# The last 16 rows of four late stores, sent apart from the other 112, in an attention backward kernel

## The chip, the core and the metric

The kernel runs on one core of one Trainium2 chip. The metric is device time in microseconds (us) for one execution, and the median of several runs counts. A core has five engines that run instructions (TensorE = PE, VectorE = DVE, ScalarE = ACT, GpSimd = POOL, SyncE = SP), and 16 DMA engines that move data between the chip's HBM and its on-chip memory SBUF, which has 128 rows (partitions). This document calls one DMA engine a **lane**.

## What is computed

Attention for one query per head, forward and backward, with 2 x 32 = 64 heads, 8,192 keys of 128 elements each, all bf16. The forward pass is

```
scores = jnp.einsum("bhqd,bhkd->bhqk", q, k) * scale
p = _softmax(scores, axis=-1)
return jnp.einsum("bhqk,bhkd->bhqd", p, v)
```

and the reference returns its output and the gradients for q, k and v from `jax.vjp`, given `grad_out`. With one query per head the gradients of K and V are outer products, as large as K and V themselves: for each head 2 MB of K and 2 MB of V are read, and 2 MB of dK and 2 MB of dV are written. In all, 268 MB are read and 268 MB are written.

## The kernel before

**Tiles.** One tensor of one head (8,192 x 128 bf16, 2,048 KB) lies in SBUF as 128 rows of 16 KB each, and in HBM it is seen in the same way (`k_v`, `dk_v` and so on, L81 to L84). Ten such places form a ring (L108). A load fills a place with K or V (L121, issued by SP). Later VectorE writes the gradient over the loaded data (`outer`, L317: four pieces for each place), and a store sends the place to HBM; then the next load can use it.

**Order.** The loop runs over heads h and, within one head, over eight steps j. While TensorE transposes K and V of head h (L144), ScalarE copies the transposed pieces out of PSUM (L151) and TensorE forms the scores (L160). In the same steps the outer products of the head before, p = h - 1, are made and stored: dV of p (w = 0) is stored in step j = 3 and dK of p (w = 1) in step j = 7, by L448. The order of each engine's instructions is that of the program text (`tc.manual_schedule`).

**Which queue stores.** As long as loads remain to be issued (`todo`) or p is under LAST = 60, ACT issues the store. From head 60 on, SP does:

```
store(p, j // 7, by=nc.scalar if todo or p < LAST else nc.sync)
```

So (60, 0), (60, 1), (61, 0), (61, 1) and (62, 0) go from SP as whole stores of 128 rows (L361). dK of head 62 and both gradients of head 63 go in halves by `store_half` (L365), each 128 rows of 8 KB. The last outputs, `out_0` and dq, are two small stores by ACT (L498).

**Six other stores** (`is_rare`, L134: every tenth store of a head, up to head 55) are cut into small transfers that POOL issues (`store_by_fifteen`, L335). A transfer of 44 rows (rows 52 to 95) comes first; then, four times, come 3 rows (L348, from rows 20 to 31), 4 rows (L349, from rows 0 to 15), 8 rows (L350, from rows 96 to 127), 4 rows (L351, from rows 32 to 47) and 2 rows (L354, from rows 16 to 19 and 48 to 51). Transfers of a few bytes (`turn`, L326) lie between them. Beside each of five of these stores, SP issues one transfer of a single row of 32 bytes (`between`, L114).

**Semaphores.** Each DMA issued by SP or ACT signals its end on one of eight semaphores, which the framework gives out in turn. The trace shows their numbers: 100, 102, 103, 104, 115, 116, 117, 118. The framework puts a wait ahead of an issue whose semaphore may still belong to an earlier DMA in flight.

Of the kernel before, what the change touches and what calls it, by code (L numbers as in the profile page):

```python
# [23 lines left out]
RING = 10  # L24
AWAY = 10
LAST = 60


@with_exitstack
def kernel(  # L30
# [11 lines left out]
    nc = tc.nc  # L42
    B, H, Sq, D = q.shape
    Sk = k.shape[2]
    P = nc.NUM_PARTITIONS
# [37 lines left out]
    dk_v = out_2.rearrange("b h (p n) d -> (b h) p n d", n=NT)  # L83
    dv_v = out_3.rearrange("b h (p n) d -> (b h) p n d", n=NT)  # L84
# [17 lines left out]
    heads = [Head() for _ in range(BH)]  # L102
# [9 lines left out]

    def between(out):
        nc.sync.dma_start(out=out, in_=q_rows[0:1, 0:16])  # L114

    todo = [(h, w) for h in range(BH) for w in range(2)]

# [5 lines left out]
    def cleared(h, w):  # L123
        for a in away:
            a[0] -= 1
        if is_rare(h, w):
            away.append([AWAY, heads[h].kv[1 - w]])
        elif todo:
            load(heads[h].kv[1 - w])
        if todo and away and away[0][0] == 0:  # L130
            between(spare[0:1, 480:496])
            load(away.pop(0)[1])

    def is_rare(h, w):  # L134
        return (2 * h + w) in range(RARE // 2, RARE * len(EXTRA), RARE)
# [199 lines left out]
    def store_by_fifteen(h, w):  # L335

        dst, src = (dv_v, dk_v)[w][h], heads[h].kv[1 - w]

        def rows(lo, n, step=4, size=8192):
            own = slice(lo, lo + step * (n - 1) + 1, step)  # L340
            nc.gpsimd.dma_start(out=dst[own], in_=src[own], max_dma_last_dim=size)  # L341

        rows(52, 44, 1)
        turn(5)
        for r, e in enumerate(EXTRA[(2 * h + w) // RARE]):
            rows(20 + r, 3)  # L348
            rows(r, 4, size=16384)  # L349
            rows(96 + r, 8)  # L350
            rows(32 + r, 4, size=16384)  # L351
            if e:
                turn(e)
            rows(16 + r, 2, step=32)  # L354
            for n in (9, 8) if e == 2 else ((3 - e) % 16,):
                turn(n)

    def store(h, w, a=0, b=NT, by=None):
        if is_rare(h, w):
            return store_by_fifteen(h, w)  # L360
        (by or nc.scalar).dma_start(  # L361
            out=(dv_v, dk_v)[w][h][:, a:b, :], in_=heads[h].kv[1 - w][:, a:b, :]
        )

    def store_half(h, w, i):  # L365
        store(h, w, 2 * i * CH, 2 * (i + 1) * CH, nc.sync)
# [22 lines left out]
    for i in range(2):  # L389
# [3 lines left out]
            out=qz[i][:, 0 : 4 * BH].rearrange("p (h z) -> p h z", z=4)[:, :, 3], in_=tps[:]  # L393
# [7 lines left out]
    with tc.manual_schedule():  # L401
        for place in ring:
            load(place)
        for h in range(BH):
# [5 lines left out]
            for j in range(NS):  # L410
# [35 lines left out]
                if x and j in (3, 7) and not (last and j == 7):  # L446

                    store(p, j // 7, by=nc.scalar if todo or p < LAST else nc.sync)  # L448
                    cleared(p, j // 7)
# [15 lines left out]
        h, x = BH - 1, heads[BH - 1]  # L465
# [64 lines left out]
```

## Time and profile before

| what | value |
|---|---|
| three runs | 1280.69, 1276.09, 1275.3 us; median 1276.09 us |
| the profiled execution | 1275.3 us, of which the span of its instructions is 1273.5 us |
| busy share of the span | PE 85%, PE weight loads 57%, DVE 70%, ACT 76%, POOL 8% |
| DMA | 44,552 packets, 539.01 MB, mean 423 GB/s |
| packets on SP's queue (q1), ACT's (q10), POOL's (q0) | 20,026, 16,736, 7,648 |
| loads, median from issue to landing | 38.8 us (K), 38.6 us (V) |
| whole stores by SP (5), from issue to landing | 20.3 us |
| half stores by SP (6), from issue to landing | 10.7 us |

The span runs from the first instruction to the last. "Landing" is the moment when a DMA's semaphore is complete. The trace has sixteen landing marks for each such DMA, one for each lane, so that it can be seen how far the lanes are apart. It also has a record of each packet (start, duration, size, queue), without the number of the lane. In a busy lane the next packet starts 3 or 4 ns before the recorded end of the one before, and with this the packets can be linked into sixteen chains.

### The profile page before, as it was taken

To read this page: it belongs to the slowest core of one execution; us is meant where nothing else is said; L and a number is where in the kernel's file an instruction comes from. 1 tells how busy PE (TensorE), PEld (TensorE's weight loads), DVE (VectorE), ACT (ScalarE), POOL (GpSimd) and SP (SyncE) were. 2 spreads that over 40 slices of the span, in tenths; PEclk is the share of its full clock that TensorE was granted. 3 is DMA by queue.
4 is the path that set the end of the run, shared out by engine and by line. 5 is a ranking of instruction groups with operands and counts; after the bars stand their busy time and mean duration, and the time that the engine had idled before them with its cause. 6 is when DMAs were issued, how large, how long until landed. Compare 5 with 4: busy or idle time off the path is not lost.

```text
span 1273.5 us, 31594 instructions
## 1 busy us (share of the span) xinstructions
PE 1083.4 (85%) x13444; PEld 721.0 (57%) x13444; DVE 891.6 (70%) x1574; ACT 971.1 (76%) x1134; POOL 106.9 (8%) x194
## 2 busy tenths in 40 slices
PE   5999998769988869888888888888888888898895
PEld 4666665546655546555565555555555555565563
DVE  1888886658766658776667677677676776776685
ACT  5898886758877759777778777777786777787785
POOL 1001110001110000211000121000111000022000
PEclk9999998889998989899889998999898999898997
DMA  9999999999999999999999999999999999999997
GB/s 393 419 428 429 425 427 427 428 430 428 426 426 426 430 429 427 427 427 426 430 429 427 430 426 426 428 429 428 426 424 426 426 428 429 425 414 426 428 415 333
DMA packets 44552, 539.01 MB, mean 423 GB/s; under 512 B 10682, under 2 KB 10682, under 8 KB 10682
## 3 DMA queue, kind: packets, MB, share of 16 engines
q1 hardware_dynamic: 20026, 285.22, 52.7%
q10 hardware_dynamic: 16736, 239.15, 44.2%
q0 software_dynamic: 7648, 12.61, 2.6%
q8 instruction: 105, 1.72, 0.5%
q14 instruction: 37, 0.30, 0.1%
HBM read 268.47 MB, written 268.47 MB: 422 GB/s over the span
## 4 chain that ended last, share of the span: by engine, by line
DMA 75%; PE 16%; ACT 4%; DVE 3%; issue 1%; ACTq 0%; SPq 0%; DVEq 0%
DMA ring<-in_k_dram 51%; DMA ring<-in_v_dram 15%; PE tp L144 9%; DMA out_dram<-ring 7%; ACT ev L151 4%; PE raw L160 2%; PE acc L285 2%; DVE ring L317 2%; PE turned L177 2%; DMA spare<-in_q_dram 1%; DMA nat<-in_grad_out_dram 1%; DVE rawsb L171 1%; DVE ev L149 0%; PE misc L229 0%; ACT E_f L218 0%
## 5 line engine op out<-in xcount | busy, mean ns | idle before, releaser
L151 ACT CAST ev<-tp 128x1024 bf16<-128x1024 f32 x960 | 936.3, 1017 | 288.4 <-PE tp L144 237.8
L144 PE MATMUL tp<-ident_bf,ring 128*128 128x128 bf16 x8192 | 661.0, 226 | 151.0 <-DMA ring<-in_k_dram 67.4
L144 PEld LDWEIGHTS <-ring 128*128 128x128 bf16 x8192 | 516.2, 101 | 370.1 <-issue 239.8
L317 DVE TENSOR_TENSOR ring<-qd,dS 128x2048 bf16<-128x2048 bf16 (+1 forms) x256 | 305.4, 1214 | 0.3 <-PE acc L285 0.3
L317 DVE TENSOR_TENSOR ring<-qd,P 128x2048 bf16<-128x2048 bf16 x255 | 305.3, 1218 | 0.1
L171 DVE COPY rawsb<-raw 128x512 f32<-128x512 f32 x127 | 87.8, 692 | 236.2 <-PE raw L160 235.0
L285 PE MATMUL acc<-ring,wz 128*32 128x512 bf16 x2048 | 211.2, 404 | 1.4 <-DVE wz L232 1.4
L160 PE MATMUL raw<-ev,qz 128*4 128x512 bf16 x2048 | 205.1, 390 | 0.1
L341 POOL DMA_DIRECT2D out_dram<-ring x126 | 70.7, 562 | 959.8 <-DVE ring L317 610.8
L177 PE MATMUL turned<-ident_f,rawsb 128*128 128x128 f32 x512 | 90.7, 305 | 11.6 <-DVE rawsb L171 10.2
L149 DVE CAST ev<-tp 128x1024 bf16<-128x1024 f32 x64 | 78.4, 1225 | 16.3 <-PE tp L144 15.7
L160 PEld LDWEIGHTS <-qz 128*4 128x4 bf16 x2048 | 46.6, 81 | 56.4 <-issue 6.2
L177 PEld LDWEIGHTS turned<-ident_f,rawsb 128*128 128x128 f32 x512 | 60.6, 154 | 26.7 <-DVE rawsb L171 25.3
L285 PEld LDWEIGHTS <-wz 128*32 128x32 bf16 x2048 | 52.7, 93 | 30.6 <-issue 3.0
L229 PEld LDWEIGHTS misc<-ld,ones_f 128*128 128x128 f32 x256 | 38.6, 190 | 15.2 <-DVE ld L256 10.9
L229 PE MATMUL misc<-ld,ones_f 128*128 128x1 f32 x256 | 46.1, 249 | 0.4 <-DVE ld L256 0.4
L209 DVE TENSOR_REDUCE gm<-misc 1x1 f32<-1x128 f32 x64 | 17.8, 279 | 38.5 <-PE misc L207 38.5
L331 POOL DMA_DIRECT2D spare<-in_q_dram x56 | 33.0, 588 | 120.3 <-DMA out_dram<-ring 102.3
L203 DVE TENSOR_REDUCE mp<-turned 128x1 f32<-128x64 f32 x64 | 14.1, 220 | 25.1 <-PE turned L177 23.9
L215 DVE TENSOR_SCALAR negm<-misc 128x1 f32<-128x1 f32 x64 | 9.8, 153 | 24.1 <-PE misc L213 24.1
L213 PE MATMUL misc<-gm,ones_f 1*128 1x1 f32 x128 | 24.2, 256 | 0.0
L213 PEld LDWEIGHTS misc<-gm,ones_f 1*128 1x128 f32 x128 | 18.7, 183 | 6.8 <-issue 0.4
(46 smaller groups left out, 283.1 us busy)
## 6 DMA issues: line engine op xcount, KB each, us to landing
out_dram<-ring ACTq DMA_DIRECT2D x114, 2048.0 KB, 19.3
ring<-in_k_dram SPq DMA_DIRECT2D x64, 2048.0 KB, 38.8
ring<-in_v_dram SPq DMA_DIRECT2D x64, 2048.0 KB, 38.6
out_dram<-ring SPq DMA_DIRECT2D x5, 2048.0 KB, 20.3
out_dram<-ring SPq DMA_DIRECT2D x6, 1024.0 KB, 10.7
out_dram<-ring POOLq DMA_DIRECT2D x6, 704.0 KB, 15.2
out_dram<-ring POOLq DMA_DIRECT2D x48, 64.0 KB, 21.1
out_dram<-ring POOLq DMA_DIRECT2D x24, 128.0 KB, 22.3
```

The lines of the kernel that those rows point to most:

```text
L144: nc.tensor.matmul(tp[:, i, :], lhsT=x.kv[w][:, n, :], rhs=ident_bf[:], start=True, stop=True)
L149: nc.vector.tensor_copy(out=ev[:], in_=tp[:])
L151: nc.scalar.copy(out=ev[:], in_=tp[:])
L160: nc.tensor.matmul(raw[32 * k : 32 * k + 4, :], lhsT=qz[w][:, at : at + 4], rhs=evs[k // 2][:, 4 * (k % 2) : 4 * (k % 2) + 4, :].rearrange ...
L171: copy(out=x.raw[:], in_=raw[:])
L177: nc.tensor.transpose(out[:, i], x.raw[:, i * P : (i + 1) * P], ident_f[:])
L213: nc.tensor.matmul(mb, lhsT=ones_f[0:1, :], rhs=x.gm[:], start=True, stop=True)
L229: nc.tensor.matmul(x.lsum, lhsT=ones_f[:], rhs=x.ld[:, w : w + 1], start=True, stop=True)
L285: nc.tensor.matmul(acc[32 * g : 32 * g + 32, :], lhsT=wz[w][:, n // 4, at : at + 32], rhs=rows[:, n : n + 4, :].rearrange("p n d -> p (n d)"),
L317: nc.vector.tensor_tensor(out=x.kv[1 - w][:, n : n + size, :].rearrange("p n (d t) -> p n d t", t=2), in0=row.unsqueeze(1).to_broadcast([P ...
L331: nc.gpsimd.dma_start(out=two(spare[0:n, :])[:, :, i : i + 2], in_=two(q_rows[0:n, :])[:, :, 0:2])
L341: nc.gpsimd.dma_start(out=dst[own], in_=src[own], max_dma_last_dim=size)
```

## The change

The stores of heads 60 and 61 by SP (four in all) no longer go as one transfer of 128 rows. Rows 0 to 111 go as one transfer, and rows 112 to 127 follow in small ones: dV (w = 0) in four transfers of four rows each, dK (w = 1) in two transfers of eight rows each. The rows of one small transfer lie 4 or 2 rows apart (112, 116, 120, 124 for the first of dV). All are issued by SP, directly behind one another. The bytes and everything else stay as they are.

```diff
+UNEVEN = {(60, 0): 4, (60, 1): 8, (61, 0): 4, (61, 1): 8}
...
+    def in_parts(engine, out, in_, n):
+        engine.dma_start(out=out[: P - 16], in_=in_[: P - 16])
+        step = 16 // n
+        for i in range(step):
+            own = slice(P - 16 + i, P, step)
+            engine.dma_start(out=out[own], in_=in_[own])
...
     def store(h, w, a=0, b=NT, by=None):
         if is_rare(h, w):
             return store_by_fifteen(h, w)
-        (by or nc.scalar).dma_start(
-            out=(dv_v, dk_v)[w][h][:, a:b, :], in_=heads[h].kv[1 - w][:, a:b, :]
-        )
+        dst, src = (dv_v, dk_v)[w][h], heads[h].kv[1 - w]
+        if (h, w) in UNEVEN:
+            in_parts(by, dst, src, UNEVEN[h, w])
+        else:
+            (by or nc.scalar).dma_start(out=dst[:, a:b, :], in_=src[:, a:b, :])
```

## Prediction

> **What bounds the kernel.** I read the page first. The DMA row is full in nearly every slice:
>
> ```profile
> DMA  9999999999999999999999999999999999999997
> GB/s 393 419 428 429 425 427 427 428 430 428 426 426 426 430 429 427 427 427 426 430 429 427 430 426 426 428 429 428 426 424 426 426 428 429 425 414 426 428 415 333
> DMA packets 44552, 539.01 MB, mean 423 GB/s; under 512 B 10682, under 2 KB 10682, under 8 KB 10682
> ```
>
> The bytes bound the span, and the change moves as many. It touches only what SP issues from 1218.8 us on, when all loads are issued (the last at 1211.0). Nothing waits for those stores but the end of the program, so the question is when the last lane is done. The stretches of the tail (columns: stretch, length, busy us of PE, PEld, DVE, ACT, POOL, clock, DMA share, GB/s):
>
> ```profile
> 1230.00:1240.00 10.00, 9.39 (x119) 6.64 (x119) 7.36 (x16) 8.92 (x12) 0.00 (x0) 1.00 0.99 419
> 1240.00:1245.00 5.00, 5.00 (x74) 2.91 (x71) 4.93 (x9) 4.36 (x6) 0.00 (x0) 1.00 0.71 301
> 1245.00:1255.00 10.00, 8.62 (x106) 5.43 (x104) 8.71 (x17) 8.48 (x15) 0.00 (x0) 1.00 0.98 412
> 1255.00:1260.00 5.00, 2.03 (x18) 0.67 (x18) 4.61 (x8) 4.97 (x19) 0.00 (x0) 0.70 0.77 321
> 1260.00:1267.00 7.00, 2.29 (x10) 1.96 (x10) 2.08 (x4) 2.02 (x8) 0.00 (x0) 0.50 1.02 426
> 1267.00:1274.00 7.00, 0.00 (x0) 0.00 (x0) 0.00 (x0) 0.00 (x0) 0.00 (x0) 0.50 0.31 124
> ```
>
> At 1240 to 1245, 1255 to 1260 and after 1267 the share falls: some lanes are out of work while others are behind. The sixteen landing marks tell which. The last load (issued 1211.0) lands in five lanes at 1218.64 to 1221.64, in three at 1223.17 to 1226.05, and in eight at 1230.45 to 1233.43. The last half store (issued 1261.53) lands in eight lanes at 1267.56 to 1267.79 and in the eight others at 1270.55 to 1272.50. That last mark ends the span 1.0 us later, at 1273.5. The eight late lanes never pause after 1218: the slowest goes from 1233.43 in steps of 4.8 to 4.9 us per whole store and 2.4 to 2.5 per half. The eight early ones do: the half store issued at 1258.87 lands there 3.7 us later, so they stood idle. A row of 16 KB takes 611 ns in a lane (median of 17,024 packets on q1).
>
> **What a late lane gains.** A whole store gives each lane 8 rows, one of 112 rows gives 7 (112 = 16 x 7). Over four stores a lane without extras saves 4 x 0.611 = 2.44 us: the slowest would land at 1270.06. The 64 rows set free go to the lanes that carry the small transfers.
>
> **Which lanes carry them** is the main choice, since no 4- or 8-row transfer from SP stands in this trace. The nearest rows are POOL's. I linked the packets of the last rare store into chains. Each transfer of n rows ran in n lanes, one row in each, and always in the same lanes: 4 rows (L349, L351) in a set F, 3 rows (L348) in a set T, 8 rows (L350) in a set E, all disjoint. One lane N got none. Of the five most early lanes 2 are of F, 1 of T and 2 of E; the next three are the other 2 of F and N; the eight late ones are 2 of T and 6 of E. SP's own one-row transfer (L114) ran all five times, the last at 1046.2 us, in one of the most early lanes. I take it as the first lane, and the order of the lanes as that of the rows: F (rows 0 to 15), N, T (20 to 31), E (96 to 127). Then a 4-row transfer fills F, and an 8-row one fills F, N and T. In rows over four stores, F gets 28 + 4 + 2 + 4 + 2 = 40, N and T get 28 + 2 + 2 = 32 as before, E gets 28.
>
> [...]
>
> So the six late lanes of E gain 2.44 us, but **the two late lanes of T gain nothing**. In the marks of the last half store these two stand at 1271.87 and 1270.55. That leaves 1272.50 - 1271.87 = 0.63 us of gain.
>
> **What the extra issues cost SP.** Four issues become 16. Two issues in a row are 0.40 us apart (1218.84 and 1219.24), so 12 x 0.40 = 4.8 us, hidden under SP's waits for VectorE: only stores stand behind them, and the window from 1205 shows
>
> ```profile
> SPq L361 <- DVE ring L317: 27.8, 8, 9.3
> ...
> SPq L361 <- DMA ring<-in_k_dram: 7.4, 1, 7.4
> ...
> SPq L361 <- DMA ring<-in_v_dram: 4.0, 1, 4.0
> ```
>
> The lower two lines matter more. A store has no use for a load of another head: (60, 0) waits for the load issued at 1179.24, because both use semaphore 102. The eight semaphores go round in order, so 16 issues take two rounds, and the new ones meet loads in flight. I follow them. (60, 0): main part 1218.84 [102], parts at 1219.2 [103], 1223.7 [104, held by the load that lands at 1223.65], 1224.1 [115], 1228.6 [116, load landing 1228.54]. (60, 1): main part 1229.0 [117] in place of 1219.24, parts 1233.5 [118, load landing 1233.43] and 1233.9 [100]. (61, 0) needs 102 again, thus the landing of the first main part in the slowest lane, 1233.43 + 7 x 0.611 = 1237.71: issued 1237.8 in place of 1227.02, its parts to 1239.4. (61, 1): 1242.1 in place of 1233.87 (one more main part, 4.28 us later). (62, 0) waits for (61, 0), last in the slower T lane with its 7 + 9 + 7 rows: about 1246.9 in place of 1243.58. From the half store at 1250.35 on, data are late again and all is as before.
>
> Does this starve a lane? An idle lane's first packet comes 0.83 us after the issue (1243.58 to 1244.41), and the mark 0.35 us after the last packet. The late lanes: the first of them ends its (60, 1) rows at 1230.1 + 14 x 0.611 = 1238.65, and the next main part is there at 1237.8 + 0.83 = 1238.63; so none pauses. The F lanes do wait, until 1238.6. From there they have 7 + 4 + 7 + 2 = 20 rows (12.2 us), the 8 of (62, 0) (4.9 us) and six halves (2.47 us each, 14.8 us) without a pause: 1238.6 + 31.9 + 0.35 = 1270.9 instead of 1267.6. They use up their slack, and stay 1.0 us below the T lane.
>
> **Sum.** Last marks: E 1270.06, F 1270.9, T 1271.87. The end moves by -0.63 us: span 1272.9, and the profiled execution's 1275.3 becomes 1274.7. The median of the runs shown is 0.8 us above that execution, so I predict 1276.09 - 0.6 = 1275.5 us. About 0.5% (6.4 us) is what a measurement of this kernel can tell from no change, so this is within it.
>
> [...]
>
> **Rivals.**
> (a) The 8-row transfers fall on the eight early lanes alone, or the T lanes are not as late as I read them. Then all late lanes gain 2.44 us and the end is F's 1270.9: -1.6 us, 1274.5. If moreover the semaphores hold nothing up, F ends at about 1270.2 at most: -2.3, 1273.8. For it: the marks split eight to eight. Against it: the chains.
> (b) Nothing moves: the small transfers are spread over all 16 lanes, 32 rows' worth in each as before. 1276.1. For it: no SP transfer of 4 rows has been seen; against it: POOL's.
> (c) **Slower: the rows cost more.** With 7 rows in each lane a lane no longer reads the same SBUF rows as in a whole store, and two lanes may meet in one group of rows. Price per row from the nearest packets: 0 from POOL's 2-row transfers, which ran in foreign lanes (of all 1,152 packets of 8 KB on q0, 7 took over 330 ns against 309); 19 ns from lane N, the slowest, whose mean is 630 ns; 407 ns if each were like the longest one at 1245 to 1260 (1,018 ns). Times 28 rows (32 in T): 0, +0.6 and up to +13 us. It decides from 0.63/32 = 20 ns per row on. I take 0, the packets that did just this; as a case of its own, 100 ns, +3 us net, 1279. [...]
> (d) Slower too: the extra rows fall on a late lane, 40 rows in place of 32, +4.9 us at its end, 1281. Against it: L114's lane was early five times.
>
> **Chances.** Forecast 0.52, (a) 0.17, (b) 0.08, (c) 0.13, (d) 0.07, other 0.03. The three runs spread over 5.4 us, so a median may lie 2 us off. The range 1272.8 to 1280.2 holds forecast, (a), (b) and most of (c). Faster by over 0.5% (below 1269.7) 0.02; slower by over 0.5% (above 1282.5), from the far ends of (c) and (d), 0.06; within 0.92.
>
> **What would show it.** q1 grows by 64 packets to 20,090 (each small transfer adds a 4-byte packet per lane it uses) at equal MB. SP's issue times are those listed; (61, 0) near 1237.8 confirms the semaphores. Four-row transfers have landing marks of four early lanes. The last half store's latest mark is near 1271.9, two lanes unmoved and six 2.4 us earlier. The row packets stay at 611 ns. I am wrong if the latest mark is below 1271 (a), at 1272.5 (b), or if the median packet of the main parts is above 630 ns (c).

## The result, and the profile after

The changed kernel takes **1292.49 us** (median of 6 runs, 1292.01 to 1293.06) against 1275.28 us before (6 runs, 1275.07 to 1280.69): a ratio of 1.0127, 95% interval 1.0111 to 1.0143, or 17.2 us slower. The forecast was 1275.5 us, the range ended at 1280.2. The profiled execution has a span of 1290.6 us.

The page of the changed kernel, the rows that answer to the first ones shown of before:

```profile
DMA  9999999999999999999999999999999999999976
GB/s 395 421 428 427 427 425 427 428 432 425 427 428 427 428 429 428 428 426 426 429 429 428 428 426 427 429 428 428 422 425 428 427 428 429 416 426 424 417 264 267
DMA packets 44616, 539.01 MB, mean 418 GB/s; under 512 B 10746, under 2 KB 10746, under 8 KB 10746
...
q1 hardware_dynamic: 20090, 285.22, 52.5%
```

The bytes are the same and q1 has the 64 packets more that were forecast. The loss is all in the last two slices, at 264 and 267 GB/s. The stretches of the tail in the changed kernel (columns as in the prediction):

```profile
1230.00:1240.00 10.00, 9.54 (x123) 6.72 (x124) 7.36 (x15) 8.85 (x11) 0.00 (x0) 1.00 0.88 304
1240.00:1245.00 5.00, 5.00 (x75) 2.96 (x73) 4.93 (x9) 4.42 (x5) 0.00 (x0) 1.00 0.96 324
1245.00:1255.00 10.00, 8.62 (x103) 5.40 (x100) 8.71 (x17) 8.48 (x16) 0.00 (x0) 1.00 0.75 242
1255.00:1260.00 5.00, 1.10 (x17) 0.34 (x16) 4.61 (x8) 4.97 (x19) 0.00 (x0) 0.80 0.24 56
1260.00:1267.00 7.00, 2.30 (x10) 1.96 (x10) 1.80 (x4) 1.75 (x7) 0.00 (x0) 0.50 0.03 7
1267.00:1274.00 7.00, 0.00 (x0) 0.00 (x0) 0.00 (x0) 0.00 (x0) 0.00 (x0) 0.50 0.90 337
1274.00:1280.00 6.00, 0.00 (x0) 0.00 (x0) 0.00 (x0) 0.00 (x0) 0.00 (x0) 0.50 1.00 421
```

Read the last two columns against each other. Two things are wrong here, and they look different. From 1230 to 1245 the lanes are busy (0.88 and 0.96) but move little for it (304 and 324 GB/s; before, 419 at a share of 0.99 and 301 at 0.71): **busy and slow**. From 1255 to 1267 they are **idle** (0.24, then 0.03), while before they were at 0.77 and 1.02; the compute engines finish as they did before. The stores that should fill this stretch come after 1267, when nothing else is left to do.

Why they come late is in the waits of SP's queue in the changed kernel, from 1205 us on (columns: waiting line, what it waited for: us in all, times, longest):

```profile
SPq L125 <- DMA out_dram<-ring: 10.8, 2, 7.1
SPq L125 <- DMA out_dram<-rows: 10.5, 1, 10.5
...
SPq L376 <- DMA out_dram<-rows: 0.2, 1, 0.2
```

L125 is a small part of a store, and it waits 10.5 us for a store of `rows`: one of the two last small stores (`out_0` and dq) that ACT issues. The trace gives the numbers. ACT's two stores, issued at 1264.46 and 1265.32, carry semaphores 103 and 104. SP's last small part of (61, 1) also needs 103: it is issued at 1266.24, behind the landing of ACT's store at 1266.23. (62, 0) needs 104 and goes at 1267.14 (before: 1243.58), and the six half stores stand behind it in SP's queue, issued from 1267.59 to 1273.50 instead of 1245.85 to 1261.53. The last lands at 1289.36.

The framework had given ACT's two stores their numbers amid SP's: SP's issues at 1238.93 and 1239.32 carry 102 and 115, and 103 and 104, which lie between, went to ACT. Before, the same could be seen: SP's stores at 1258.87, 1259.61 and 1261.53 have 102, 104 and 116, and ACT's two have the missing 103 and 115. But only two SP issues stood behind the first of them there, and the turn of eight did not come round. In the changed kernel fourteen do. ACT's stores take two of the eight numbers, so six SP issues go by before the turn comes back to ACT's two, and the other eight are held behind them: one small part, (62, 0) and six halves. The twelve added issues do not do this by their count, since all of them stand ahead of the half stores, among which ACT's numbers fell before: **the place of ACT's two numbers in the turn has moved forward.**

The "busy and slow" part is in the packets: a row of 16 KB on q1 takes a mean of 738 ns from 1218 to 1262 us (the longest 2,688) against 616 before (the longest 1,102).

So there are two theories beside the forecast. **W**, the hold: stores wait in SP's queue for ACT's last two. **R**, the rows: a transfer of 112 rows makes rows dear (G and S below are forms of it, N its rival). A third suspect, the twelve extra issues themselves, is tested too (theory I in the expectations).

### The profile page after: what moved, and what is told of

Its sections match the earlier page's. It is cut to its first block, busy times and chain, and to the rows that moved or that the text cites. A ratio compares the mean times of both kernels' runs of the same rounds, so it can differ in the third digit from the quotient of the medians.

```text
span 1290.6 us, 31608 instructions
## 1 busy us (share of the span) xinstructions
PE 1089.5 (84%) x13444; PEld 722.3 (56%) x13444; DVE 891.1 (69%) x1574; ACT 971.9 (75%) x1134; POOL 106.9 (8%) x194
## 3 DMA queue, kind: packets, MB, share of 16 engines
q1 hardware_dynamic: 20090, 285.22, 52.5%
## 4 chain that ended last, share of the span: by engine, by line
DMA 72%; PE 17%; ACT 4%; DVE 3%; issue 1%; ACTq 0%; SPq 0%; DVEq 0%
DMA ring<-in_k_dram 54%; DMA ring<-in_v_dram 11%; PE tp L155 9%; DMA out_dram<-ring 7%; ACT ev L162 4%; PE acc L296 3%; PE raw L171 3%; DVE ring L328 2%; PE turned L188 2%; DMA nat<-in_grad_out_dram 1%; DVE rawsb L182 1%; PE misc L240 0%; DVE ev L160 0%; ACT E_f L229 0%; PE misc L314 0%
## 5 line engine op out<-in xcount | busy, mean ns | idle before, releaser
L328 DVE TENSOR_TENSOR ring<-qd,P 128x2048 bf16<-128x2048 bf16 x255 | 305.3, 1218 | 0.1
L188 PE MATMUL turned<-ident_f,rawsb 128*128 128x128 f32 x512 | 88.5, 299 | 11.5 <-DVE rawsb L182 10.1
L240 PEld LDWEIGHTS misc<-ld,ones_f 128*128 128x128 f32 x256 | 38.6, 190 | 15.3 <-DVE ld L267 11.6
```

The source lines that it names most:

```text
L188: nc.tensor.transpose(out[:, i], x.raw[:, i * P : (i + 1) * P], ident_f[:])
L240: nc.tensor.matmul(x.lsum, lhsT=ones_f[:], rhs=x.ld[:, w : w + 1], start=True, stop=True)
L328: nc.vector.tensor_tensor(out=x.kv[1 - w][:, n : n + size, :].rearrange("p n (d t) -> p n d t", t=2), in0=row.unsqueeze(1).to_broadcast([P ...
```

## The experiments

Medians are compared with runs of the kernel before that were made with them on the same chip (median 1275.36 to 1275.59). Only the edits are shown; those marked "from the change" start from the changed kernel, the others from the kernel before.

### The hold: rows_by_sp, before_rows_by_sp, head60_only, fours_only

**rows_by_sp**, from the change, lets SP issue the last two small stores itself, behind all others; **before_rows_by_sp** does so in the kernel before.

```diff
-            nc.scalar.dma_start(out=dst, in_=rows[:])
+            nc.sync.dma_start(out=dst, in_=rows[:])
```

> The changed kernel, with the two last small stores (out_0 and dq) issued by SP behind its half stores instead of by ACT. Theory W (SP's store waits for ACT's two small stores because they were given the semaphore numbers 103 and 104 before SP's later stores came to them): no store of SP has to wait for them now, the half stores are issued when their data are ready (1250 to 1261.5), and the 10.5 us wait is gone; with rows of 611 ns the time is 1274.7 us. Theory R (the rows of a 112-row transfer cost more: packets of 16 KB took 707 ns on average from 1218 to 1245 in the changed kernel, 616 in the one before) acting beside W: up to 28 rows times 0.17 us, 1280. R alone, or theory I (twelve more issues on SP hold the queue by themselves): the time stays at 1288 or more, and the gap in the DMA share from 1255 to 1267 stays.

> The kernel before with the same move of the two small stores to SP: the control for the run with the changed kernel. All theories: within 1.5 us of the kernel before (1275.3), a little slower, since the two small stores now stand behind the last half store in SP's queue.

Measured: rows_by_sp 1282.37 us, ratio 1.0052 [1.0035, 1.0068]; before_rows_by_sp 1275.4 us, 0.9996 [0.9986, 1.0005]. The edit by itself does nothing, and takes 10.1 us off the changed kernel (1292.49 to 1282.37). The same stretches in rows_by_sp:

```profile
1230.00:1240.00 10.00, 9.54 (x127) 6.62 (x125) 7.33 (x17) 8.52 (x11) 0.00 (x0) 1.00 0.98 333
...
1255.00:1260.00 5.00, 1.38 (x16) 0.34 (x16) 4.62 (x8) 4.97 (x19) 0.00 (x0) 0.67 0.89 285
1260.00:1267.00 7.00, 2.30 (x10) 1.96 (x10) 1.46 (x4) 1.32 (x6) 0.00 (x0) 0.50 1.00 420
```

The empty stretch from 1255 to 1267 is gone: W is right. The slow one is still there, 333 GB/s at a share of 0.98, and 6.8 us remain (1282.37 - 1275.59); R had allowed for less, up to 1280 us.

The 10.1 and the 6.8 us are not the prices of two separate costs. With the hold, the lanes had run dry before 1267 (a share of 0.03), so nearly all that slow rows had cost by then was hidden under it. An estimate for the hold alone, with the prediction's own terms: (62, 0) is issued at 1267.14, when ACT's store allows it, and 1267.14 + 0.83 + 4.9 + 14.8 + 0.35 = 1288.0 for the last landing, against 1289.36 measured. The hold alone would thus make about 16 of the 17.2 us; take it away, and 6.8 us of slow rows come into view. No run has the hold without the 112-row transfers.

**head60_only** and **fours_only**, from the change, cut only two of the four stores, so that fewer issues stand behind ACT's numbers.

```diff
-UNEVEN = {(60, 0): 4, (60, 1): 8, (61, 0): 4, (61, 1): 8}
+UNEVEN = {(60, 0): 4, (60, 1): 8}     # head60_only
+UNEVEN = {(60, 0): 4, (61, 0): 4}     # fours_only
```

> The change for head 60 alone: six more issues in place of twelve. In the program the semaphores of ACT's two small stores come round again at the last two half stores of SP. Theory W: these two are issued only when ACT's small stores have landed, about 1266.2 and 1267.1 in place of 1259.6 and 1261.5; the lanes are empty by then, 0.83 + 2 x 2.47 + 0.35 us later the end is near 1272.6, so the time is 1274 to 1277 though the wait is there. Theory I: half of the loss, 1284. Theory R: half of the row price, at most 1278, and no store is held up.

> The change for the two dV stores alone (8 more issues, all of four rows). The semaphores of ACT's small stores come round at the first half store of head 63, so the last four half stores of SP are held. Theory W: they are issued from 1266.2 on, and four half stores of 2.47 us end at 1266.2 + 0.83 + 9.9 + 0.35 = 1277.3, 4.8 us later than before: 1280. Theory I: two thirds of the loss, 1287. Theory R: half the row price, 1276 to 1279, with no store held.

Measured: 1278.8 us (1.0027 [1.0017, 1.0037]) and 1283.59 us (1.0047 [1.0019, 1.0075]). The hold shrinks with the number of issues, but it is still there: two half stores are held in head60_only, issued at 1270.29 and 1270.77, four in fours_only, issued from 1266.28 to 1268.88. That fits the count: eight and ten SP issues stand behind ACT's numbers there, and six go by in each. Both times are above what W alone had forecast (at most 1277, and 1280), so here too something else costs. From head60_only's waits of SP's queue:

```profile
SPq L376 <- DMA out_dram<-rows: 11.7, 1, 11.7
```

Here ACT's store was issued at 1264.03 and had landed in fifteen lanes by 1267.52, but in the sixteenth at 1270.22; SP went on at 1270.29. That one lane, 2.7 us behind the other fifteen, held both half stores.

### The issues: tiny_twelve

The kernel before with whole stores, and twelve transfers of 32 bytes by SP at the places of the small parts.

```diff
+        for i in range({(60, 0): 4, (60, 1): 2, (61, 0): 4, (61, 1): 2}.get((h, w), 0)):
+            at = 16 * len(tiny)
+            tiny.append(at)
+            nc.sync.dma_start(out=small[0:1, at : at + 16], in_=q_rows[0:1, 0:16])
```

> The kernel before, with whole stores, and twelve transfers of 32 bytes more on SP at the places of the changed kernel's small transfers (4, 2, 4 and 2 behind the stores of heads 60 and 61). In this program the numbers of ACT's two small stores fall late, and none of SP's stores comes back to them. Theory W and theory R: no hold and no slow row; SP issues its stores later by the turn of the semaphores alone, within 1.5 us of the kernel before. Theory I (the number of issues): the 7 us that remained with the small stores on SP, or more, so 1282 or later.

Measured: 1276.29 us, ratio 1.0007 [0.9998, 1.0016]. Twelve issues and their turn of semaphores cost 0.9 us, no more than the measurement can tell from nothing. ACT's stores have the numbers 117 and 100 here, and two SP issues stand behind the first of them, as before. So the count of issues does not move ACT's place. It stays at two in main_only, seven_eighths, col_halves and by_columns below as well; it moves in every kernel that adds row transfers of 16 KB a row and leaves ACT's stores to ACT. There six SP issues stand behind it in row_halves, even_odd, the two crossed kernels and sixteens (so none is held by ACT's stores), and eight, ten and fourteen in head60_only, fours_only and the change. How the framework chooses the place is not shown. The whole stores went out at 1229.26, 1239.17, 1243.69 and 1248.54; the prediction had 1229.0, 1237.8, 1242.1 and 1246.9 by following the semaphores.

### The rows: main_only, seven_eighths, sixteens

**main_only** issues the 112-row transfers alone. **seven_eighths** leaves out as many bytes the other way: all 128 rows, 56 of 64 columns. **sixteens** sends the 16 rows as one transfer, by count one row for each lane. All are from the change.

```diff
         engine.dma_start(out=out[: P - 16], in_=in_[: P - 16])
-        step = 16 // n
-        for i in range(step):
-            own = slice(P - 16 + i, P, step)
-            engine.dma_start(out=out[own], in_=in_[own])      # main_only: no more than the line above
-        engine.dma_start(out=out[: P - 16], in_=in_[: P - 16])
+        engine.dma_start(out=out[:, :56, :], in_=in_[:, :56, :])     # seven_eighths: this alone
-UNEVEN = {(60, 0): 4, (60, 1): 8, (61, 0): 4, (61, 1): 8}
+UNEVEN = {(60, 0): 16, (60, 1): 16, (61, 0): 16, (61, 1): 16}     # sixteens
```

> Only the 112-row transfers: rows 112 to 127 of the four stores are left out (64 rows of 16 KB are not written), so there is no extra issue and no wait for ACT's small stores. If a row of a 112-row transfer costs no more than one of a whole store, each lane does 4 rows less, 2.44 us, and the time is 1272.9. Theory R (0.17 us more per row, from the packet durations of the changed kernel): 28 x 0.17 = 4.8 us more than that, 1277 to 1278, and from 1224 to 1245 the DMA share stays near 1 while the rate falls from 419 to about 330 GB/s.

> The control for the run with 112 rows alone: the same four stores move the same number of bytes, but as 128 rows of which each leaves out its last eighth (14 KB of 16 KB; what is left out is not written). No theory gives it a row price: 1272.9, packets of 14 KB in about 0.54 us, and a rate above 410 GB/s up to 1240. Theory R is that the difference between the two runs is the price of 112 rows; without R they are equal.

> The same split, but the last 16 rows go as one transfer in all 16 lanes, so each lane keeps its 8 rows; 4 more issues, and no store comes back to the semaphores of ACT's small stores. Without a row price: 1275.3, as before. Theory R: 28 rows of the main parts at 0.17 us more, +4.8, and the 16-row transfers more per row than that, since all of their rows lie close together in SBUF: 1280 to 1288. Theory W alone: 1275.3.

Measured: main_only 1285.21 us (1.0074 [1.0059, 1.0089]), seven_eighths 1273.61 us (0.9987 [0.9977, 0.9996]), sixteens 1287.27 us (1.0081 [1.0063, 1.0099]). With the same bytes and the same four issues, **the shape of 112 rows costs 1285.21 - 1273.61 = 11.6 us**. R's forecast for main_only, 1277 to 1278 us, was some 7 us short: it had spread the price evenly over the lanes. The stretches of main_only, then those of seven_eighths:

```profile
1230.00:1240.00 10.00, 9.54 (x128) 6.57 (x125) 7.33 (x17) 8.37 (x11) 0.00 (x0) 1.00 0.97 331
...
1245.00:1255.00 10.00, 8.18 (x99) 5.24 (x95) 8.72 (x17) 8.49 (x16) 0.00 (x0) 1.00 0.97 292
```

```profile
1230.00:1240.00 10.00, 9.30 (x122) 6.59 (x119) 7.36 (x16) 8.92 (x12) 0.00 (x0) 1.00 0.90 377
...
1245.00:1255.00 10.00, 8.78 (x109) 5.50 (x105) 8.72 (x15) 8.49 (x14) 0.00 (x0) 1.00 0.97 406
```

At a share of 0.97 in both, one moves 292 GB/s and the other 406. In main_only the loss falls on two lanes: the last half store lands in fourteen lanes from 1271.5 to 1273.9, in the two others at 1278.54 and 1282.55. It was also held up itself: SP waited 7.0 us for its semaphore, until the slowest lane of (62, 0) had landed, at 1267.73 (before: 1257.70).

### Which rows: row_halves, even_odd, col_halves, by_columns

Theory G says that lanes slow each other when, in a transfer of another shape than a whole store's, they read SBUF rows that lie together; which rows lie together was my supposition, shown by no run. The test cuts each of the four stores in two, by rows, by every second row, and by columns; by_columns makes the change's twelve small transfers out of columns.

```diff
+        for own in (slice(0, 64), slice(64, 128)):                    # row_halves
+        for own in (slice(0, 128, 2), slice(1, 128, 2)):              # even_odd
+            engine.dma_start(out=out[own], in_=in_[own])
+        for own in (slice(0, 32), slice(32, 64)):                     # col_halves
+            engine.dma_start(out=out[:, own, :], in_=in_[:, own, :])
+        engine.dma_start(out=out[:, :48, :], in_=in_[:, :48, :])      # by_columns
+        step = 16 // n
+        for i in range(step):
+            own = slice(48 + i * n, 48 + (i + 1) * n)
+            engine.dma_start(out=out[:, own, :], in_=in_[:, own, :])
```

> Each of the four stores goes as two transfers of 64 rows, rows 0 to 63 and then rows 64 to 127: 4 issues more than before, every row stored, rows of 16 KB as in a whole store, and in each transfer 4 rows for each of 16 lanes. No store meets a number that one of ACT's last small stores holds. [...] Theory N (only a row number that is no power of two, 7 for each lane, is dear, or only the small transfers): 1275.5 us.

> As with the two row halves, but the two transfers of a store hold its even and its odd rows. [...] A weaker form of G, in which it only matters that a transfer as a whole spreads over all rows: about as before, below 1279 us. Theory N: 1275.5 us.

> The control to the two row halves: each of the four stores goes as two transfers of all 128 rows, columns 0 to 31 and 32 to 63, packets of 8 KB; 4 issues more than before, all bytes stored. Each lane keeps its 8 rows. Theory G and theory N: 1275.5 us, 8 KB packets near 309 ns. If it is only the number of larger transfers that costs, it is as slow as the row halves.

> The change's scheme with the cut laid the other way: of each of the four stores, columns 0 to 47 of all 128 rows go as one transfer and columns 48 to 63 follow in four transfers of four columns (dV) or two of eight (dK): the same 12 extra issues by SP, behind the same ones, all bytes stored, each lane with its own 8 rows in every transfer. No store meets a number of ACT's last small stores. Theory G: 1275.5 to 1277 us. If many transfers between the stores are what costs, whatever their rows: 1282 us and more.

Measured: row_halves 1287.9 us (1.0101 [1.0084, 1.0118]), even_odd 1275.64 us (1.0001 [0.9992, 1.001]), col_halves 1275.93 us (1.0005 [0.9996, 1.0014]), by_columns 1276.12 us (1.0003 [0.9994, 1.0012]). The stretch in row_halves, then in even_odd:

```profile
1245.00:1255.00 10.00, 9.03 (x116) 5.75 (x114) 8.72 (x15) 8.44 (x13) 0.00 (x0) 1.00 1.00 345
```

```profile
1245.00:1255.00 10.00, 8.29 (x99) 5.26 (x95) 8.72 (x17) 8.49 (x17) 0.00 (x0) 1.00 0.98 411
```

Theory N falls: four rows for each lane are as dear as seven when they lie in one half. Theory G has row_halves right (12.3 us slower), but it had even_odd slow as well, and that costs nothing (1.0001); only its weaker form has both right. So the rows taken matter, and **my picture of which rows lie together was wrong**. And by_columns has the very number and places of issues of the change, at no cost: neither the issues nor the small transfers are dear by themselves.

### Read or written: halves_to_even_odd, even_odd_to_halves

The two good cuts and the two bad ones differ on both sides, in the SBUF rows read and the output rows written. These cross them.

```diff
+        for i in range(2):                                            # halves_to_even_odd
+            engine.dma_start(out=out[i:128:2], in_=in_[64 * i : 64 * i + 64])
+        for i in range(2):                                            # even_odd_to_halves
+            engine.dma_start(out=out[64 * i : 64 * i + 64], in_=in_[i:128:2])
```

> As the two row halves, but the rows are written elsewhere: SBUF rows 0 to 63 of each of the four stores go to the even rows of the output, rows 64 to 127 to the odd ones, so these four stores hold the right rows in the wrong places. If the dear side is the SBUF rows that are read: 1286 to 1290 us, as the row halves (1287.9). If it is the output rows that are written: 1275.6 us, as even and odd rows were.

> The other crossing: even SBUF rows go to the upper half of the output rows, odd ones to the lower half (right rows in the wrong places, in the four stores). If the SBUF side is dear: 1275.6 us. If the output side is: 1286 to 1290 us. If both of the crossed kernels are slow, or neither, it needs both sides together.

Measured: 1287.19 us (1.0086 [1.0072, 1.01]) and 1275.47 us (1.0 [0.9991, 1.0009]). The stretch in halves_to_even_odd, then in even_odd_to_halves:

```profile
1245.00:1255.00 10.00, 8.20 (x99) 5.26 (x95) 8.72 (x17) 8.49 (x16) 0.00 (x0) 1.00 0.98 326
```

```profile
1245.00:1255.00 10.00, 8.70 (x109) 5.50 (x105) 8.72 (x17) 8.49 (x14) 0.00 (x0) 1.00 0.98 415
```

Again one share, 0.98, and two rates. The rate follows the SBUF rows that are read, wherever they are written: **the dear side is the SBUF**.

### Groups of rows, and the change done the other way: strided_main, strided_change, row_quarters, every_fourth

What fits so far is theory S, a supposition too: each lane must stay in its own stretch of eight consecutive rows. If the lanes take the rows of a transfer in order, which no run shows, strided_main gives each lane seven rows of its stretch, and strided_change, which adds the rest in small transfers, is the change as it was meant. row_quarters and every_fourth send four transfers of 32 rows for each store. In all four SP issues ACT's last two stores, as in rows_by_sp.

```diff
+        for own in (slice(0, 128, 2), slice(1, 128, 4), slice(3, 128, 8)):    # strided_main
+            engine.dma_start(out=out[own], in_=in_[own])
+        for i in range(16 // n):                                      # strided_change: these too
+            own = slice(7 + 8 * i, 128, 128 // n)
+            engine.dma_start(out=out[own], in_=in_[own])
+            own = slice(32 * i, 32 * i + 32)                          # row_quarters, i from 0 to 3
+            own = slice(i, 128, 4)                                    # every_fourth, i from 0 to 3
```

> Seven rows for each lane, all from its own stretch of eight: each of the four stores goes as the even rows (64), rows 1, 5, 9 and so on (32) and rows 3, 11, 19 and so on (16), all of 16 KB; rows 7, 15, 23 and so on are left out, as rows 112 to 127 were where 112 rows went in one transfer (1285.2 us). ACT's two last small stores go by SP, so that no number is held. Theory S (a lane must stay in its stretch of eight rows): 1273.5 to 1275.5 us, packets at 611 ns. Theory N (seven rows for each lane are dear as such): 1283 us and more.

> The change with its rows taken the other way, and nothing left out: as the kernel with seven rows for each lane, and rows 7, 15, 23 and so on follow in four transfers of four rows (dV) or two of eight (dK); ACT's two last small stores go by SP. It has 20 issues more than before. If my prediction was right but for the price of the rows and the hold: the six late lanes gain up to 2.4 us, two do not, 1273.5 to 1276.0 us. If the extra issues or waits cost by themselves: above 1277 us. If small transfers of rows that lie far apart are as dear as the 112 rows: 1280 us and more.

> Each of the four stores goes as four transfers of 32 consecutive rows (12 issues more than before), ACT's two last small stores by SP so that no number is held; every row is stored. Each lane has 2 rows in each transfer. Theory S (groups are stretches of eight consecutive rows): four lanes meet in each of four groups, in step a lane runs at a quarter of its rate, twice as bad as the row halves: 1295 to 1320 us, many packets near 2,400 ns. [...]

> The control to the quarters: each of the four stores goes as rows 0, 4, 8 and so on, then 1, 5, 9 and so on, and so forth: also four transfers of 32 rows, 12 issues more, ACT's two last small stores by SP, every row stored. Theory S: each lane has two rows of its own stretch in each transfer, 1275.5 to 1277 us. If the count of row transfers or their semaphores cost by themselves, as the slow strided_change may say: above 1279 us.

Measured: strided_main 1276.49 us (1.0006 [0.9997, 1.0015]), strided_change 1280.66 us (1.0036 [1.0024, 1.0049], 1279.61 to 1286.68), row_quarters 1282.76 us (1.0056 [1.0039, 1.0073]), every_fourth 1276.15 us (1.0004 [0.9995, 1.0013]). The stretch in row_quarters, then in every_fourth:

```profile
1245.00:1255.00 10.00, 8.62 (x104) 5.44 (x101) 8.71 (x17) 8.49 (x15) 0.00 (x0) 1.00 0.98 308
```

```profile
1245.00:1255.00 10.00, 8.43 (x99) 5.26 (x96) 8.72 (x17) 8.48 (x16) 0.00 (x0) 1.00 1.02 427
```

every_fourth has the same 16 transfers of 32 rows by SP as row_quarters, spread over all rows, and it costs nothing. But S forecast 1295 us and more for the quarters, above the 1282.76 measured. The packets of 16 KB on q1 from 1218 to 1262 us, by kernel:

| kernel | mean ns | 90% below, ns | over 900 ns | longest, ns |
|---|---|---|---|---|
| before | 616 | 620 | 0.5% | 1,102 |
| even_odd | 619 | 624 | 0.7% | 1,187 |
| even_odd_to_halves | 618 | 620 | 0.7% | 1,178 |
| every_fourth | 619 | 627 | 0.6% | 1,182 |
| strided_main | 647 | 662 | 4.3% | 1,846 |
| strided_change | 683 | 892 | 9.5% | 2,225 |
| row_halves | 705 | 1,105 | 15% | 1,513 |
| halves_to_even_odd | 714 | 1,108 | 15% | 2,680 |
| main_only | 740 | 1,194 | 17% | 2,601 |
| the change | 738 | 1,124 | 17% | 2,688 |
| row_quarters | 765 | 1,251 | 22% | 2,631 |
| sixteens | 787 | 1,256 | 25% | 2,885 |

The median is 611 to 612 in every one of these; what grows is the share of packets over 900 ns, from 0.5% before to 25% in sixteens, where the longest took 2,885. Two lanes at half rate would need 2 x 611 = 1,222 ns for a row (an estimate; in the six dearest kernels 90% lie below 1,105 to 1,256). Sharing would look like that, though no run shows it or settles which rows share.

strided_main misses S's forecast of at most 1275.5 us by 1.0 us, and is 2.9 us slower than seven_eighths with as many bytes; its packets are longer as well (4.3% over 900 ns). strided_change is 5.2 us slower than before. In its profile the lanes have little to do from 1230 to 1240:

```profile
1230.00:1240.00 10.00, 9.31 (x126) 6.35 (x125) 8.73 (x11) 9.14 (x12) 0.00 (x0) 1.00 0.52 178
```

SP waited there for two loads whose numbers the parts of (60, 0) needed (landed at 1233.65 and 1238.56), and (60, 1) began at 1239.18. With seven transfers for a dV store and eight semaphores, the next store soon needs a number of the one ahead of it (SP's issue at 1241.19 follows the landing of (60, 0)'s first transfer in its slowest lane, at 1241.17). That this is the whole of the 5.2 us is argued, not shown. The profiled execution was also the longest of the seven, 6.0 us above their median, and it ran late before the change could act: its last load was issued at 1214.25 (before: 1211.00) and (60, 0) at 1223.95 (before: 1218.84). No version tried with all rows stored beats the kernel before clear of noise.

## Why the prediction was wrong

**What held.** The lanes bound the tail, the bytes stay, q1 grew to 20,090 packets. The hidden cost of the issues held: tiny_twelve adds 0.9 us and by_columns 0.5, both inside their intervals. (In the change itself a small part's issue took 0.58 to 3.10 us, not the 0.40 counted.) The turn of the semaphores held up to (61, 0): (60, 1) went out at 1229.00 as forecast, its parts at 1233.26 and 1233.96 (1233.5 and 1233.9), (61, 0) at 1238.93 (1237.8; its predecessor's slowest lane was 0.8 us late, with dear rows). From there on it did not: (61, 1) went out at 1247.64, not 1242.1, because with 103 and 104 given away a part of (61, 0) needed 117, the number of (60, 1)'s main part, which landed in its slowest lane at 1246.30. Three of the four-row transfers of (60, 0) landed before the late lanes of its main part (by 1231.17, 1232.39 and 1233.61, the late lanes from 1234.27; the fourth, issued at 1228.37, by 1234.66), which fits a set F of early lanes. The forecast's 40, 32 and 28 rows also need 8-row transfers in F, N and T. No run shows that: it was an estimate from POOL's chains and the order of the rows, and the marks do not name their lanes. What a late lane gains can be seen only in seven_eighths, where every lane has an eighth less to move: 1.7 us (0.5 to 2.9 by the interval) against the 2.44 forecast. Even that, with every late lane relieved, is a small sum beside what follows.

**First failed step: "From the half store at 1250.35 on, data are late again and all is as before."** I followed the eight semaphores along SP's own order of issue and left out their other user. Two numbers went to ACT's last two stores, which are not issued until 1264.46 and 1265.32. The missing 103 and 115 in SP's numbers stood in the trace of before, two issues from the end. In the changed kernel they are fourteen from the end, and everything after the sixth is held: seven stores and one small part. Taking the hold away gains 10.1 us (the change against rows_by_sp). None of the rivals named it. The extra issues did not cost by their own time or their count (tiny_twelve, by_columns), but with these row transfers among them the framework gave ACT its numbers early, and that was the dear part.

**Second failed step: rival (c), "I take 0".** The prediction named the cause, rows that cost more, and its point of decision (20 ns a row), and the nearer rows decided for the wrong end. POOL's 2-row transfers ran in foreign lanes at no price, but they occupied two lanes at a time, and they are only 96 of the 1,152 packets quoted for it, of which 7 took over 330 ns (96 = 6 stores x 4 transfers x 2 rows x 2 packets). In a 112-row transfer, if it is dealt in sevens in the order of the rows, nearly all lanes at once would read other rows than in a whole store (argued: the trace has no row numbers). The measured mean is 122 ns more (738 - 616), and it does not fall evenly: with the hold away it costs 6.8 us in the change, 11.6 us in main_only where two lanes take most of it. The upper end, "up to +13 us", came from the one row that showed a long packet, and it was the better guide. Rival (c) had a chance of 0.13 and a price of 3 us from 100 ns a row, so the size was wrong as well: put on the 512 rows of the four stores alone, the excess of the changed kernel is some 190 ns a row (an estimate: 849 packets x 117 ns from 1218 us on, over 512). The prediction's sign for (c), a median packet above 630 ns, would have missed it too: the median of q1 stays at 611, and the price lies in the 17% of packets over 900 ns.

Either failure alone would have put the time beyond the forecast: with no hold it is 1282.4, and with the hold alone some 16 us above 1275, by the estimate above.

**What stays open.** Which SBUF rows slow each other when they are read at the same time, and how the chip deals out the rows of a transfer with a step. Neither G nor S forecast all of it: 112 rows, 64 and 32 consecutive rows (11.6, 12.3 and 7.4 us), every second and every fourth row (0.1 and 0.8 us, free within their intervals), and 64 + 32 + 16 rows with a step (nearly free, 2.9 us above seven_eighths). Two things on record speak against S. In its stretches strided_main's third transfer (rows 3, 11, 19 and so on) is even like the others, and its packets would not have grown, yet 4.3% of them took over 900 ns. And by the prediction's chains POOL's rows 0 to 15 and 32 to 47 ran in the same four lanes. Those rows are four stretches of eight, so by S at least half of them were outside a lane's own stretch; yet of their 192 packets of 16 KB only 2 took over 700 ns. It is a lead and not a finding: no run tells in which order a lane takes its rows.

What moves ACT's place in the turn of the semaphores is open as well.

## What to carry to other kernels

When issues are added to a queue, follow the turn of semaphores over all engines that share them, to the end of the program and in the changed program, since the places can move: a gap in one queue's numbers is another engine's DMA, and if that is issued late, what comes round to its number waits for it (10.5 us in the change). Take a store of SBUF rows whole, or cut it by columns or by every second or fourth row (ratios of 1.0001 to 1.0005 here); 112, 64 or 32 consecutive rows at a time cost 7 to 12 us over four stores of 2 MB here. And in the table of stretches read the DMA share and the GB/s as a pair: in the change, a share of 0.03 at 7 GB/s was stores not yet issued; in main_only, a share of 0.97 at 292 GB/s was rows that took longer.

## What the hardware showed that I had not expected

In stores that went as 112, 64 or 32 consecutive SBUF rows at a time, a row of 16 KB took a mean of 740, 705 and 765 ns (main_only, row_halves, row_quarters) against 616 before, and a single one up to 2,885 (sixteens) against a median of 611. Between even_odd_to_halves and row_halves only the choice of SBUF rows differs, and 15% of the packets take over 900 ns in place of 0.7%.

An issue by SP is not always short. A whole store's took 332 ns before; in the changed kernel four of SP's issues took 1,988 to 3,096 ns, in rows_by_sp up to 3,428, in row_quarters up to 3,341. In every_fourth, with as many issues, transfers and rows, none of the sixteen took over 1,128. So it is not the number of issues; that it goes with lanes that are behind is what the runs have in common, and why is not shown.

A single late lane held a queue. A whole store has sixteen landing marks, and in main_only the next user of its number waited for the last of them: 7.0 us, with fifteen lanes done 4 us earlier (1263.72) than the sixteenth (1267.73).
